# A fused attention and expert kernel: the two layers of each expert run back to back, and rows are loaded three experts ahead

## The chip, the cores and the metric

One core of a Trainium2 chip runs the whole program. The metric is the device time of one execution in microseconds (us), lower is better. TensorE is called PE in the profile (PEld is its weight load), VectorE DVE, ScalarE ACT, GpSimd POOL and SyncE SP.

## The reference

Three stages follow one another; the change touches the third.

```python
def _moe2_ref(x, w_skip, w_gate, w1, w2):      # x: 2304 tokens x 512, 8 experts, w1 512x1024, w2 1024x512
    do_compute = x @ w_skip > 0
    out = x.copy()
    xc = x[do_compute]
    logits = xc @ w_gate
    e_idx = np.argmax(logits, axis=1)
    probs = ...                                 # softmax of logits
    gate_w = probs[np.arange(len(xc)), e_idx]
    for e in range(E):
        mask = e_idx == e
        h = np.maximum(xc[mask] @ w1[e], 0.0)
        y[mask] = gate_w[mask, None] * (h @ w2[e])
    out[do_compute] = xc + y
    return out

def reference(**kwargs):
    attn_out = _attn_ref(...)                   # attention of 4 batches, 8 heads, local and strided masks
    x = _moe_ref(x=attn_out, w_in, w_out)       # x @ w_in, gelu-like gate, @ w_out
    return _moe2_ref(x=x, ...)
```

## The kernel before

The attention and the dense layer fill the first 585 us of the trace, with the routing of each group of tokens behind its dense layer. The routing scatters every token's row (512 numbers, its gate and its token number) by an indirect DMA of POOL into `xs_d` (L709), in a bin of 160 rows for its expert, and its number into a table (L710). The second stage, from about 585 us on, is the expert stage, and the change lies in it.

**One expert** e has five kinds of work. `load_x(e)` (L926) reads its 160 rows back from `xs_d`, as two halves of 80 rows, by two DMAs of SP (L929); each waits until the scatters have landed. `emit_X(e, cp)` (L933) transposes them on PE (L940), four transposes of 80 rows for each half `cp` of the columns, and DVE copies the result out to `xs[e]` (L944). `emit_L1(e, m)` (L946), for m of 0 to 7, multiplies with `w1` (L954) into a PSUM tile, and ACT takes the ReLU to `hT[e]` (L955). `emit_L2(e, c)` (L957), for c of 0 to 3, multiplies `hT[e]` with `w2` over its eight blocks (L963), and DVE copies the result to `yT[e]` (L966). `emit_Y(e)` (L968) transposes back on PE (L973), DVE multiplies by the gate and adds the row (L975), and POOL scatters the result rows to the output by an indirect DMA (L978). In the program's text each float32 product of L954 or L963 is one matmul; in the trace it is two, so that a layer of an expert is 32 products or 64 traced matmuls. Expert 0 has no `emit_X`: its rows are built on PE out of what is on the chip already (`xs0`).

**Weights.** A layer's weights are four loads of 512 KB on SP's queue (L202 for `w1`, L204 for `w2`). `wseq` (L183) is the order of the layers, and `wjobs` numbers the 64 loads by it, from 0 to 63; `wfill` (L208) issues them some layers ahead (`WD = 5`). Each goes into one of 33 buffers that the earlier stages use too. From load 14 on (`LG = 14`) a load is issued behind the first row loads (`issue_after`, L199).

**Order.** The lines emit the work in program order, and a scheduler then places instructions of each engine by its own estimate of times, so that the order on an engine can differ from the text. Before the change `wseq` is layer 1 of expert 0, layer 1 of expert 1, layer 2 of expert 0, layer 1 of expert 2, layer 2 of expert 1 and so on: layer 2 of an expert stands behind layer 1 of the next. The loop at L1005 walks through it; behind L1 piece 1 of expert e it emits `emit_Y(e - 2)` and `load_x(e + 2)`, and behind pieces 4 and 6 the two halves of `emit_X(e + 1)`. The rows of experts 1, 0, 2 and 3 are loaded ahead of the loop (L1000 to L1003).

Of the kernel before, what the change touches and what calls it, by code (L numbers as in the profile page):

```python
# [19 lines left out]
E, FF = 8, 1024  # L20
# [43 lines left out]
def attn_moe_moe_kernel(ctx: ExitStack, tc: tile.TileContext, q, k, v, w_in, w_out, w_skip, w_gate, w1, w2, out):  # L64
# [115 lines left out]
            wo[i] = w.rearrange("p (h n) -> p h n", h=2)  # L180


    wseq = [(0, 0)]  # L183
    for e_ in range(E):
        if e_ + 1 < E:
            wseq.append((e_ + 1, 0))
        wseq.append((e_, 1))
    wjobs = [(e_, l_, i_) for e_, l_ in wseq for i_ in range(4)]
    wx = {}
    nx = [0]  # L190
# [17 lines left out]
    def wfill(n):  # L208

        while nx[0] < min(n, len(wjobs)):  # L210
            wx_load()
# [3 lines left out]
    def after_scatters(ins, l_):  # L215

        for o_ in l_[SF - 1 :]:
            tc.add_manual_dep(
                ins, o_.ins.name, mybir.DependencyInfo(mybir.DependencyClass.Sync, mybir.DependencyReason.DATA), reason="every scatter has landed"
            )  # L220
# [701 lines left out]
    with ExitStack() as ph2:  # L922
# [3 lines left out]
        def load_x(e):  # L926
            for h in range(2):
                t = mp.tile([128, DM + 2], F32, tag="xr", bufs=8, name="xr")
                xl.append(nc.sync.dma_start(out=t[0:HC, :], in_=xs_d[e * CAP + h * HC : e * CAP + h * HC + HC]))  # L929
                after_scatters(xl[-1].ins, scat)  # L930
                xr[e, h] = t

        def emit_X(e, cp):  # L933

            if cp == 0:
                xs[e] = mp.tile([128, NC, CAP], F32, tag="xs", name="xs")
            tp = ps.tile([128, 2, CAP], F32, tag="t", bufs=2, name="tx")
            for c in range(2):
                for h in range(2):
                    nc.tensor.transpose(  # L940
                        out=tp[:, c, HC * h : HC * h + HC], in_=xr[e, h][0:HC, 128 * (2 * cp + c) : 128 * (2 * cp + c) + 128],
                        identity=ident[0:HC, 0:HC],
                    )
            nc.vector.tensor_copy(xs[e][:, 2 * cp : 2 * cp + 2, :], tp)  # L944

        def emit_L1(e, m):  # L946
            if m == 0:

                hT[e] = [half_tile(F32, "hT")[:, 0 : 4 * CAP].rearrange("p (k n) -> p k n", k=4) for _ in range(2)]
            tag = L1T0[m] if e == 0 else ("h", "sc", "h", "pv")[m % 4]  # L950
            p = ps.tile([128, CAP], F32, tag=tag, bufs=2 if tag == "h" else 1, name="h1")
            for c in range(NC):
                x = xs[e][:, c] if e else xs0[0][:, c]
                nc.tensor.matmul(out=p, lhsT=wx[e, 0, c][:, 128 * m : 128 * m + 128], rhs=x, start=(c == 0), stop=(c == NC - 1))  # L954
            nc.scalar.activation(out=hT[e][m // 4][:, m % 4, :], in_=p, func=AF.Relu)  # L955

        def emit_L2(e, c):  # L957
            if c == 0:
                yT[e] = mp.tile([128, NC, CAP], F32, tag="yT", name="yT")
            p = ps.tile([128, CAP], F32, tag=L2T[c] if e >= E - 2 else f"acc{c % 2}", bufs=2 if e >= E - 2 and L2T[c] == "h" else 1, name="h2")  # L960
            for k_ in range(NF):
                o = 512 * (k_ % 2) + 128 * c
                nc.tensor.matmul(  # L963
                    out=p, lhsT=wx[e, 1, k_ // 2][:, o : o + 128], rhs=hT[e][k_ // 4][:, k_ % 4], start=(k_ == 0), stop=(k_ == NF - 1)
                )
            nc.vector.tensor_copy(yT[e][:, c, :], p)  # L966

        def emit_Y(e):  # L968
            res = mp.tile([HC, 2, DM], F32, tag="res", bufs=2, name="res")
            for h in range(2):  # L970
                p = ps.tile([HC, DM], F32, tag="t", bufs=2, name="yp")
                for c in range(NC):
                    nc.tensor.transpose(out=p[:, 128 * c : 128 * c + 128], in_=yT[e][:, c, HC * h : HC * h + HC], identity=ident)  # L973
                xe = xr.pop((e, h))
                nc.vector.scalar_tensor_tensor(  # L975
                    out=res[:, h, :], in0=p, scalar=xe[0:HC, 512:513], in1=xe[0:HC, 0:DM], op0=ALU.mult, op1=ALU.add
                )
                ys.append(nc.gpsimd.indirect_dma_start(  # L978
                    out=out, out_offset=bass.IndirectOffsetOnAxis(ap=xe[0:HC, 513:514].bitcast(U32), axis=0), in_=res[:, h, :], in_offset=None,
                    bounds_check=NT - 1, oob_is_err=False,  # L980
                ))
                if len(ys) > 1:
                    tc.declare_no_dep(ys[-1].ins, ys[-2].ins, reason="rows of different tokens")

        seq = [(0, 0)]
        for e in range(E):
            if e + 1 < E:
                seq.append((e + 1, 0))
            seq.append((e, 1))

        pc = ps.tile([128, E], F32, tag="pv", name="pc")
        nc.tensor.matmul(out=pc, lhsT=ones, rhs=ohacc[:, 0:E], start=True, stop=True)
# [12 lines left out]
        for i, (e, layer) in enumerate(wseq):  # L1005
            n = NF if layer == 0 else NC
            for z in range(n):
                if z % (n // 4) == 0:
                    wfill(4 * (i + WD) + z * 4 // n + 1)
                if layer == 0:  # L1010
                    emit_L1(e, z)
                    if z == 1:
                        if e >= 2:
                            emit_Y(e - 2)
                        if 2 <= e < E - 2:
                            load_x(e + 2)
                    if z in (4, 6) and e + 1 < E:
                        emit_X(e + 1, z // 2 - 2)
                else:
                    emit_L2(e, z)  # L1020
                    if (e, z) == (E - 1, 0):
                        emit_Y(E - 2)
        emit_Y(E - 1)


# [88 lines left out]
```

## Time and profile before

| | us |
|---|---|
| median of 3 runs | 758.82 (757.9 to 760.88) |
| the profiled execution | 758.55 |
| its span in the trace | 756.8 |
| PE busy in the span | 715.0 (94%) |
| DVE, ACT, POOL busy | 352.9, 340.1, 164.2 |
| bytes moved by DMA | 84.44 MB |

The span is the profiled execution from its first to its last traced instruction; 1.75 us of the execution's own time lie around it. A matmul's end is modelled, and a matmul's entry reaches into the next, so the distance from one start to the next is what a matmul costs; some matmul records are missing from merged rows. The row of the clock is the granted share of TensorE's clock: 1.00 is 2.4 GHz, 0.50 is 1.2 GHz.

### The profile page before, as it was taken

The numbers are of one execution on the slowest core, as the hardware profiler recorded it, in microseconds if no ns is written. First come the engines' busy times: TensorE is split into PE (matmuls) and PEld (weight loads), VectorE is DVE, ScalarE is ACT, GpSimd is POOL, SyncE is SP. The second block draws the span as 40 slices with busy tenths as digits, with TensorE's granted clock in tenths as the row PEclk, the third lists the DMA queues.
The fourth block names the chain that finished last, engine by engine and source line by source line (L and its number), as shares of the span: only waits on it lengthen the run. The fifth ranks groups of instructions, "written<-read, shape, count | busy, mean of one in ns | idle before, by whom it ended". The sixth has DMA issues, their size and how long they took to land.

```text
span 756.8 us, 14113 instructions
## 1 busy us (share of the span) xinstructions
PE 715.0 (94%) x4945; PEld 630.5 (83%) x4945; DVE 352.9 (47%) x1450; ACT 340.1 (45%) x1098; POOL 164.2 (22%) x226
## 2 busy tenths in 40 slices
PE   5879989999999999999999999999999799999993
PEld 3558877888788888888888889989988699999993
DVE  3698986354655565366556443353453011121111
ACT  4886695663665665456665442332441111011100
POOL 5376774023031103003110302002021000000001
PEclk9968999999999999999999999999999899999998
DMA  8999921311220412211100000100792599961001
GB/s 194 340 336 289 273 53 25 84 34 45 68 52 20 108 35 34 74 33 45 50 17 1 17 30 16 57 1 16 223 161 68 180 398 397 358 231 36 16 14 33
DMA packets 99056, 84.44 MB, mean 112 GB/s; under 512 B 63508, under 2 KB 78036, under 8 KB 98976
## 3 DMA queue, kind: packets, MB, share of 16 engines
q1 hardware_dynamic: 95680, 78.39, 35.4%
q0 software_dynamic: 3296, 5.05, 2.1%
q8 instruction: 41, 0.67, 0.4%
q14 instruction: 39, 0.32, 0.2%
HBM read 71.00 MB, written 17.68 MB: 117 GB/s over the span
## 4 chain that ended last, share of the span: by engine, by line
PE 67%; issue 15%; DMA 8%; ACT 5%; DVE 2%; SPq 1%; POOL 0%; POOLq 0%; ACTq 0%; DVEq 0%
PE h L561 26%; PE acc L588 26%; DMA wx<-in_moe_w_dram 4%; PE sc L399 4%; PE pv L464 3%; PE tp L442 2%; DMA out_dram<-res,xr 2%; ACT pt L417 2%; ACT kb L337 1%; PE p L357 1%; PE tr L618 1%; DMA tab_d<-rows,ix 1%; PE lc L632 1%; PE p L361 1%; SPq L929 0%
## 5 line engine op out<-in xcount | busy, mean ns | idle before, releaser
L561 PE MATMUL h<-xT,wsp 128*128 128x256 f32 x1728 | 245.8, 287 | 2.5 <-POOL wsp L176 0.7
L561 PEld LDWEIGHTS h<-xT,wsp 128*128 128x128 f32 x1728 | 229.3, 191 | 18.3 <-issue 2.1
L588 PE MATMUL acc<-wsp,ghl 128*128 128x512 f32 x816 | 227.3, 404 | 1.0 <-ACT wsp L175 0.5
L588 PEld LDWEIGHTS acc<-wsp,ghl 128*128 128x128 f32 x816 | 141.3, 188 | 26.7 <-issue 2.0
L427 POOL TENSOR_TENSOR pt<-pt,st 96x256 f32<-96x256 f32 (+3 forms) x88 | 50.2, 589 | 241.0 <-DVE st L424 88.6
L565 DVE SCALAR_TENSOR_TENSOR g<-g,h 128x256 f32<-128x256 f32 x144 | 59.9, 418 | 89.9 <-ACT g L564 86.2
L564 ACT ACTIVATE g<-h 128x256 f32<-128x256 f32 x144 | 54.6, 382 | 96.0 <-PE h L561 88.6
L577 ACT ACTIVATE ghl<-g 128x256 fp32r<-128x256 f32 (+1 forms) x144 | 58.1, 405 | 63.2 <-DVE g L565 56.5
L954 PE MATMUL h<-xs,wx 128*128 128x160 f32 x512 | 77.5, 305 | 0.0
L417 ACT ACTIVATE pt<-pt,st 96x128 f32<-96x128 f32 (+3 forms) x176 | 67.3, 386 | 14.2 <-DVE st L409 13.9
L955 ACT ACTIVATE hT<-h 128x160 f32<-128x160 f32 x64 | 19.4, 303 | 120.7 <-PE h L954 115.1
L954 PEld LDWEIGHTS h<-xs,wx 128*128 128x128 f32 x512 | 72.8, 195 | 0.0
L963 PE MATMUL h<-hT,wx 128*128 128x160 f32 x512 | 72.4, 299 | 0.0
L578 DVE TENSOR_TENSOR ghl<-g,ghl 128x256 fp32r<-128x256 f32 (+1 forms) x128 | 53.2, 416 | 37.8 <-ACT ghl L577 29.4
L963 PEld LDWEIGHTS h<-hT,wx 128*128 128x128 f32 x512 | 70.3, 190 | 0.0
L399 PE MATMUL sc<-kb,qT 128*96 128x256 f32 (+3 forms) x220 | 45.4, 331 | 4.9 <-ACT kb L337 4.6
L709 POOL DMA_INDIRECT xs_d<-rows,ix x18 | 18.1, 1006 | 133.9 <-DVE ix L706 41.3
L176 POOL TENSOR_TENSOR wsp<-wcv,wsp 128x512 fp32r<-128x512 f32 x32 | 41.0, 1284 | 24.6 <-ACT wsp L175 24.0
L978 POOL DMA_INDIRECT out_dram<-res,xr x16 | 14.6, 914 | 145.5 <-DVE res L975 103.0
L966 DVE COPY yT<-h 128x160 f32<-128x160 f32 x32 | 10.4, 325 | 75.7 <-PE h L963 75.7
L337 ACT ACTIVATE kb<-p 64x64 fp32r<-64x64 f32 (+3 forms) x58 | 39.7, 684 | 10.7 <-DVE qT L340 3.8
L399 PEld LDWEIGHTS sc<-kb,qT 128*96 128x96 f32 (+2 forms) x220 | 32.1, 177 | 11.3 <-issue 4.5
(151 smaller groups left out, 762.0 us busy)
## 6 DMA issues: line engine op xcount, KB each, us to landing
wx<-in_moe_w_dram SPq DMA_DIRECT2D x64, 512.0 KB
wraw<-in_moe_w_in_dram SPq DMA_DIRECT2D x16, 512.0 KB
wraw<-in_moe_w_out_dram SPq DMA_DIRECT2D x16, 512.0 KB
raw<-in_q_dram SPq DMA_DIRECT2D x32, 128.0 KB
raw<-in_k_dram SPq DMA_DIRECT2D x32, 128.0 KB
out_dram<-rows SPq DMA_DIRECT2D x16, 256.0 KB
xs_d<-zinit SPq DMA_DIRECT2D x1, 2570.0 KB
xr<-xs_d SPq DMA_DIRECT2D x16, 160.6 KB
```

Of the source, the lines that this page charges most:

```text
L337: nc.scalar.activation(out=d[0], in_=ops[-1][0], func=AF.Copy)
L399: nc.tensor.matmul(out=sc[0:qn, j, :, 0:kn], lhsT=qt[a][:, q0 : q0 + qn], rhs=kt[c][:, :, k0 : k0 + kn], start=(n_ == 0), stop=(n_ == len( ...
L417: nc.scalar.activation(out=P[0:qn, j, h, 0:kn], in_=P[0:qn, j, h, 0:kn], func=AF.Exp, scale=-1.0, bias=st[0:qn, 0, i : i + 1], accum_out=s ...
L427: nc.gpsimd.tensor_tensor(out=P[0:qn, j, :, 0:kn], in0=P[0:qn, j, :, 0:kn], in1=st[0:qn, 1, 2 * j : 2 * j + 2, None].to_broadcast([qn, 2, ...
L561: nc.tensor.matmul(out=hp_, lhsT=wi[m][:, a, c, :], rhs=x[z], start=(n_ == 0), stop=(n_ == 3 * NC - 1))
L564: nc.scalar.activation(out=g, in_=hp_, func=AF.Tanh, scale=0.851)
L565: nc.vector.scalar_tensor_tensor(out=g, in0=g, scalar=1.0, in1=hp_, op0=ALU.add, op1=ALU.mult)
L577: nc.scalar.activation(out=t[:, 0], in_=g[:, a:z], func=AF.Copy)
L578: (nc.gpsimd if gi == 0 else nc.vector).tensor_tensor(out=t[:, 1], in0=g[:, a:z], in1=t[:, 0].bitcast(F32), op=ALU.subtract)
L588: nc.tensor.matmul(out=acc[gi, i], lhsT=ghl[i][:, a, :], rhs=wo[m][:, z, :], start=(m == 0 and n_ == 0), stop=(m == NM - 1 and n_ == 2),)
L954: nc.tensor.matmul(out=p, lhsT=wx[e, 0, c][:, 128 * m : 128 * m + 128], rhs=x, start=(c == 0), stop=(c == NC - 1))
L963: nc.tensor.matmul(out=p, lhsT=wx[e, 1, k_ // 2][:, o : o + 128], rhs=hT[e][k_ // 4][:, k_ % 4], start=(k_ == 0), stop=(k_ == NF - 1))
```

## The change

`wseq` becomes layer 1, layer 2 of expert 0, then both layers of expert 1, and so on; the weight loads are numbered by it. In the loop `emit_Y(e - 1)` comes behind piece 2 of layer 1 of e, and `load_x(e + 3)` behind that; the two halves of `emit_X(e + 1)` come behind pieces 1 and 2 of layer 2 of e (2 and 3 for expert 0). An unused list `seq` goes.

```diff
-    wseq = [(0, 0)]
-    for e_ in range(E):
-        if e_ + 1 < E:
-            wseq.append((e_ + 1, 0))
-        wseq.append((e_, 1))
+    wseq = [(e_, l_) for e_ in range(E) for l_ in range(2)]
...
                 if layer == 0:
                     emit_L1(e, z)
-                    if z == 1:
-                        if e >= 2:
-                            emit_Y(e - 2)
-                        if 2 <= e < E - 2:
-                            load_x(e + 2)
-                    if z in (4, 6) and e + 1 < E:
-                        emit_X(e + 1, z // 2 - 2)
+                    if z == 2 and e >= 1:
+                        emit_Y(e - 1)
+                        if e + 3 < E:
+                            load_x(e + 3)
                 else:
                     emit_L2(e, z)
-                    if (e, z) == (E - 1, 0):
-                        emit_Y(E - 2)
+                    z0 = 1 if e else 2
+                    if z0 <= z < z0 + 2 and e + 1 < E:
+                        emit_X(e + 1, z - z0)
         emit_Y(E - 1)
```

After the scheduler, the order on every engine is the same in both kernels up to the third product of expert 0's sixth group, apart from which weights the loads 4 to 13 fetch; on POOL it is the same to the end. In the rows below, `h_7327` and the like are PSUM tiles, `xs_7215` is expert 0's `xs0`, `xr` the loaded rows, `hT` the hidden layer, `x4` four products in a row.

PE, before, from the last products of expert 0's layer 1 that need no new rows to the first of layer 2:

```order
L954 MATMUL h_7321<-xs_7215,wx 128x160 x2
L954 MATMUL h_7334<-xs_7215,wx 128x160
L940 MATMUL tx<-ident,xr 128x80
L954 MATMUL h_7334<-xs_7215,wx 128x160
L940 MATMUL tx<-ident,xr 128x80 x3
L954 MATMUL h_7342<-xs_7215,wx 128x160 x4
L940 MATMUL tx<-ident,xr 128x80 x4
L954 MATMUL h_7354<-xs_7215,wx 128x160 x4
L963 MATMUL h_7446<-hT,wx 128x160
L963 MATMUL h_7434<-hT,wx 128x160
L954 MATMUL h_7364<-xs,wx 128x160 x2
```

Here the transposes of expert 1's rows (L940) stand inside the sixth group of expert 0's layer 1.

PE, after, at the same place:

```order
L950 MATMUL h_7327<-xs_7215,wx 128x160 x2
L959 MATMUL h_7362<-hT,wx 128x160
L950 MATMUL h_7335<-xs_7215,wx 128x160 x4
L959 MATMUL h_7362<-hT,wx 128x160 x2
L950 MATMUL h_7341<-xs_7215,wx 128x160 x4
L959 MATMUL h_7350<-hT,wx 128x160 x7
L959 MATMUL h_7362<-hT,wx 128x160 x4
L959 MATMUL h_7350<-hT,wx 128x160
L959 MATMUL h_7362<-hT,wx 128x160
L936 MATMUL tx<-ident,xr 128x80 x8
L959 MATMUL h_7374<-hT,wx 128x160 x8
L959 MATMUL h_7393<-hT,wx 128x160 x8
```

Now they stand behind all of that layer and half of layer 2, as one piece of eight.

SP, before, around the rows of expert 4 (a transfer waits for the semaphore that the transfer eight places ahead of it on the queue raises, `DMAHW0` to `DMAHW7` in turn):

```order
L204 DMA wx<-in_moe_w_dram 128x2x512 [waits DMAHW0_49,PE_49]
L202 DMA wx<-in_moe_w_dram 128x1024 [waits DMAHW1_49,PE_49]
L929 DMA xr<-xs_d 80x514 [waits DMAHW2_49,DMASW0_49,DVE_49]
L929 DMA xr<-xs_d 80x514 [waits DMAHW3_49,DMASW1_49,DVE_49]
L202 DMA wx<-in_moe_w_dram 128x1024 [waits DMAHW4_49,PE_49]
```

Here the rows follow 39 of the 50 weight loads that stand behind the first row loads.

SP, after, at the same place:

```order
L198 DMA wx<-in_moe_w_dram 128x1024 [waits DMAHW0_49,PE_49]
L925 DMA xr<-xs_d 80x514 [waits DMAHW1_49,DMASW0_49,DVE_49]
L925 DMA xr<-xs_d 80x514 [waits DMAHW2_49,DMASW1_49,DVE_49]
L200 DMA wx<-in_moe_w_dram 128x2x512 [waits DMAHW3_49,PE_49]
L200 DMA wx<-in_moe_w_dram 128x2x512 [waits DMAHW4_49,PE_49]
```

Now they follow 38 of them, the last of which is load 51.

PE, after, from the end of a middle expert's layer 1 to the transposes for the next expert (`h_7779` and `h_7791` are the first two pieces of layer 2):

```order
L950 MATMUL h_7764<-xs,wx 128x160 x4
L950 MATMUL h_7770<-xs,wx 128x160 x4
L959 MATMUL h_7779<-hT,wx 128x160 x6
L959 MATMUL h_7791<-hT,wx 128x160
L959 MATMUL h_7779<-hT,wx 128x160
L959 MATMUL h_7791<-hT,wx 128x160 x3
L959 MATMUL h_7779<-hT,wx 128x160
L959 MATMUL h_7791<-hT,wx 128x160 x4
L936 MATMUL tx<-ident,xr 128x80 x8
```

The scheduler has put seven and three products of other operands ahead of the two products that need the last two pieces of the hidden layer.

## Rows read from the trace of the kernel before

**Rows 1.** Windows of the span: PE busy, its clock, DMA share, GB/s

```profile
580.00:590.00 10.00, 9.44 (x72) 9.06 (x71) 3.71 (x32) 2.26 (x8) 1.94 (x2) 1.00 0.17 39
590.00:600.00 10.00, 4.35 (x26) 4.10 (x25) 0.49 (x1) 1.21 (x4) 0.00 (x0) 0.81 0.52 130
600.00:610.00 10.00, 10.00 (x70) 9.96 (x69) 0.98 (x2) 1.82 (x6) 0.00 (x0) 0.85 1.03 377
610.00:620.00 10.00, 10.00 (x77) 10.00 (x76) 1.14 (x3) 1.52 (x5) 0.00 (x0) 1.00 1.04 397
...
640.00:650.00 10.00, 10.00 (x77) 9.97 (x77) 1.73 (x3) 1.82 (x6) 1.82 (x2) 1.00 1.04 398
```

**Rows 2.** Timeline of PE: start, length, line, count, idle before and its releaser

```profile
585.69 6.41 PE L954 MATMUL h<-xs,wx 128*128 128x160 f32 x46
...
597.75 0.36 PE L940 MATMUL tx<-ident,xr 80*128 80x80 f32 x1 [5.65 <-DMA xr<-xs_d]
```

**Rows 3.** Windows of PE alone, one us each: busy, clock, DMA share, GB/s

```profile
595.00:596.00 1.00, 0.00 (x0) 1.00 0.89 294
596.00:597.00 1.00, 0.00 (x0) 0.56 0.96 208
...
601.00:602.00 1.00, 1.00 (x7) 0.50 0.96 348
602.00:603.00 1.00, 1.00 (x5) 0.53 0.98 383
603.00:604.00 1.00, 1.00 (x10) 1.00 1.05 401
```

**Rows 4.** Timeline of PE later in the stage, and the ReLU of a group

```profile
622.81 0.98 PE L954 MATMUL h<-xs,wx 128*128 128x160 f32 x6
...
623.83 0.30 ACT L955 ACTIVATE hT<-h 128x160 f32<-128x160 f32 x1 [5.08 <-PE h L954]
...
667.69 1.04 PE L973 MATMUL yp<-ident,yT 128*80 128x128 f32 x8
668.57 6.69 PE L954 MATMUL h<-xs,wx 128*128 128x160 f32 x48
675.09 0.43 PE L963 MATMUL h<-hT,wx 128*128 128x160 f32 x2
675.36 0.72 PE L940 MATMUL tx<-ident,xr 80*128 80x80 f32 x8
675.92 3.19 PE L963 MATMUL h<-hT,wx 128*128 128x160 f32 x22
...
743.78 1.04 PE L973 MATMUL yp<-ident,yT 128*80 128x128 f32 x8
```

**Rows 5.** Groups by line, whole span: count, busy, mean ns, idle before

```profile
L954 PE MATMUL h<-xs,wx 128*128 128x160 f32 x512 | 77.5, 305 | 0.0
L963 PE MATMUL h<-hT,wx 128*128 128x160 f32 x512 | 72.4, 299 | 0.0
...
L940 PE MATMUL tx<-ident,xr 80*128 80x80 f32 x56 | 6.9, 248 | 5.7 <-DMA xr<-xs_d 5.7
```

**Rows 6.** Timeline of SP: start of the first issue and time to the last

```profile
555.72 2.46 SPq L202 DMA_DIRECT2D wx<-in_moe_w_dram  x2
...
593.78 3.70 SPq L929 DMA_DIRECT2D xr<-xs_d  x8
597.52 0.90 SPq L202 DMA_DIRECT2D wx<-in_moe_w_dram  x2
...
606.82 4.43 SPq L204 DMA_DIRECT2D wx<-in_moe_w_dram  x4
...
617.36 4.42 SPq L204 DMA_DIRECT2D wx<-in_moe_w_dram  x4
...
627.92 4.46 SPq L204 DMA_DIRECT2D wx<-in_moe_w_dram  x4
...
639.17 4.43 SPq L204 DMA_DIRECT2D wx<-in_moe_w_dram  x4
644.86 0.34 SPq L202 DMA_DIRECT2D wx<-in_moe_w_dram  x1
645.80 1.61 SPq L929 DMA_DIRECT2D xr<-xs_d  x2
```

**Rows 7.** Timeline of POOL: the output scatters of expert 0 and the last

```profile
627.87 0.93 POOL L978 DMA_INDIRECT out_dram<-res,xr  x1 [40.09 <-DMA wx<-in_moe_w_dram]
...
746.99 0.91 POOL L978 DMA_INDIRECT out_dram<-res,xr  x1 [0.30 <-issue]
```

More of the change, by code (lines that the diff above doesn't have):

```diff
@@ L983, in emit_Y @@
                     tc.declare_no_dep(ys[-1].ins, ys[-2].ins, reason="rows of different tokens")
[L985 to L989, printed above, removed]
         pc = ps.tile([128, E], F32, tag="pv", name="pc")
```

## The prediction

> **What bounds the kernel now.** I read the windows of the expert stage first, then PE's timeline, then SP's. The windows [rows 1] show PE filled from 600 us on, with one hole: between 590 and 600 us it is busy 4.35 of 10 us. PE's timeline gives the hole its name [rows 2]: the products of expert 0 run dense from 585.69 to 592.1 us, then PE stands for 5.65 us until 597.75, and what releases it is the landing of expert 1's rows, for the transposes of L940 are next in its order. The groups by line show no other idle at the products or the transposes of rows [rows 5]. The hole costs more than its length. The granted clock falls to 0.50 (1.2 GHz) at about 596.4, 4.3 us after PE stopped, and comes back at about 602.9, 5.2 us after PE resumed [rows 3]. In those 5.2 us PE does 2.6 us of work. So the place is worth 5.65 + 2.6 = **8.25 us**.
>
> Beyond it the stage is PE's own work. Start to start, 48 products of L954 take from 668.57 to 675.09, 0.1358 us each; eight transposes back take 0.88 (667.69 to 668.57), eight of rows 0.56 (675.36 to 675.92) [rows 4]. So 1024 traced products, eight times 0.88, seven times 0.56 and the last drain of 0.16 (1.04 less 0.88) make 139.06 + 7.04 + 3.92 + 0.16 = 150.2 us. From 585.69 to the end of the last transposes (743.78 + 1.04 = 744.82) there are 159.1. The difference, 8.9, is the 8.25 and 0.65 of seams between groups, which I leave as they are.
>
> **Part 1: layer 2 of expert 0 moves ahead of everything that needs expert 1's rows.** The row loads themselves are not moved: SP issues them at 593.78, behind the last scatters, in both kernels. What moves is the need. After the change 64 products of layer 1 and 32 of layer 2 of expert 0 stand ahead of the first transpose: 585.69 + 96 x 0.1358 = 598.73 us. The rows were there at 597.75 at the latest, so the wait ends 1.0 us too early to be felt, and without the hole nothing lets the clock fall. Gain 8.25 us. The cover of this is expert 0's layer 2, and its weights must be there by 592 us. They are loads 4 to 7 now; the fourteenth load was issued by 558.2 [rows 6], 34 us earlier, and a load under full traffic takes 10.5 us (the issue at 617.36 waited for the one at 606.82, eight ahead of it). If they were not, the hole would be as before.
>
> **Part 2: layer 2 follows layer 1 of its own expert.** This adds a chain, PE, ReLU on ACT, PE, at eight boundaries. ACT starts 0.04 us after a group's end and takes 0.30 (622.81 + 0.98, then 623.83) [rows 4]. After a middle expert's last group eleven products, 22 traced matmuls, stand ahead of the one that reads the last piece: 22 x 0.1358 = 3.0 us of cover over some 0.4. I take nothing; without cover it would be 8 x 0.4 = 3 us. Behind the transposes of rows stand 32 matmuls, 4.3 us, ahead of the layer that reads them, so DVE's copies are covered too. What DVE, ACT and POOL execute is the same in number, and the end behind PE (the last scatter at 746.99 [rows 7]) is the same chain.
>
> **Part 3: rows three ahead.** The rows of expert 4 come by SP's queue behind load 51, and this is where the next wait stands. SP has at most eight transfers out. Loads 24 and 40 were issued at 606.82 and 627.92, a pace of 1.319 us a load; the next eight took 11.25 us instead of 10.55, and in them ran the output scatter of expert 0 (627.87), so a scatter costs the stream 0.70 [rows 6, 7]. After the change the scatters of experts 0 and 1 are done ahead of load 44's issue: 606.82 + 20 x 1.319 + 2 x 0.70 = 634.6. It lands 10.55 later, at 645.15, and lets the first half of the rows go. Seven loads are still out: 7 x 1.319 = 9.23, the scatter of expert 2 in that time 0.70, and 160.6 KB of rows against 512 KB in 1.319 us make 0.41. That is 655.5, and 655.9 for the second half. PE's need: an expert costs 8.69 + 0.88 + 8.69 + 0.56 = 18.82; expert 0 ends at 603.64; experts 1 and 2, layer 1 of expert 3 with its transposes (9.57) and half of its layer 2 (4.35) give 655.2. With 0.2 us from landing to release (SP went on at 597.52, PE at 597.75 [rows 2, 6]), PE waits about **0.9 us**, too short for the clock if 4.3 us were needed above. Before the change this place was not tight: transposes and rows were farther apart. The ends for this wait: rows that land as quickly as the first did, 3.7 us from issue (593.78 to 597.5), would be there at 650 and cost nothing; if each scatter held the stream 2 us instead of 0.7, it would be 4.8. I take the 0.9, since the stretch is the same saturated one (DMA share 1.04 at 640 to 650 us [rows 1]). Experts 5 to 7 are not tight: by the same count the rows of expert 5 land at about 669 and are needed at 675.
>
> The Trainium skill, DMA: Bandwidth & Descriptors, section "Queues, rings and completion order", speaks against the moved loads: what SP issues takes its place in the same rings, and each engine consumes a ring in order. By that rule the rows of expert 4 come behind the seven loads, as I have counted, and the sum is 751.2; if the rule did not hold here they would overtake, and the sum would be 750.3. No row of before decides it, since nobody waited for those rows there.
>
> **The sum.** The profiled execution took 758.55 us, 0.27 under the median of 758.82. 758.55 - 8.25 + 0.9 = 751.2; on the scale of the median, about **751.4 us**.
>
> **The rivals.**
> A, no new wait: the rows of expert 4 are in time, 758.55 - 8.25 = 750.3. For it: an idle queue landed rows in 3.7 us. Against: the saturated stream.
> B, the hole closes but the clock falls all the same, or a second pause near the start follows: only 5.65 is gained and 0.9 paid, 753.8. For it: the margin at expert 1's rows is 1.0 us only. Against: in the trace the clock fell only behind a pause of 4.3 us.
> C, the chain at the boundaries is not covered: the bunch of matmuls signals late, and each of eight costs 0.5: 751.2 + 4 = 755.2. Against: ACT followed its group by 0.04 us.
> D, slower: the rows of expert 4 come much later than counted, because weights and three scatters share the engines worse than in rows 6. A wait there of 5.65 us with a clock that falls again eats the whole 8.25; it decides from a landing at 660.9, 5 us later than my count. At 663 us the time is about 761 and, if expert 5 follows, 763.
> E, the change does not do what it says: the hole returns in front of layer 2 because its weights or the first rows are late, 758.5. Against: 34 us of lead, and the 1.0 us margin.
>
> **How the numbers follow.** Forecast 0.46, A 0.31, B 0.08, C 0.07, D 0.04, E 0.04. About 0.5% (3.8 us) is what a measurement of this kernel can tell from no change. The forecast, A, B and half of C are faster by more than that (below 755.0): 0.88. The other half of C and E lie within it: 0.08. D is slower: 0.04. For the range, the runs of before spread from 0.9 below to 2.1 above their median; from A less 1 to B plus 1 it is 749.2 to 754.8, and it leaves out C in part, D and E.
>
> **What would show it.** In the profile after: no idle between 585.7 and 598 us and a clock of 1.00 there and to 605; the transposes of expert 1 at about 598.7; the boundaries between layers without idle; one wait of PE on rows at about 655 us, of 0 to 2.5 us, and none at expert 5; the last PE instruction's end near 737.5 instead of 744.8. I am wrong if the clock drops between 596 and 603 without a pause, if PE waits for weights in layer 2 of expert 0, or if the wait at expert 4 is above 4 us.

## The result and the profile after

| us | before | after |
|---|---|---|
| median, runs of one session | 759.65 (757.9 to 761.4, 6 runs) | 753.6 (751.25 to 754.68, 6 runs) |
| ratio to before | 1 | 0.991 [0.9891, 0.9929] |
| the profiled execution | 758.55 | 751.34 |
| expert stage, first product to the end of the last transposes | 159.13 (585.69 to 744.82) | 152.23 (585.38 to 737.61) |
| stage less the 150.2 of work counted in the prediction | 8.9 | 2.0 |

The kernel became 0.9% faster: 751.34 in the profiled execution against 751.2 by the sum, 753.6 in the median against the forecast of 751.4, inside the range of 749.2 to 754.8. The stage gave all of it, 6.9 us between the two profiles.

The windows of 10 us of the kernel after, in the columns of [rows 1] (time, PE, PEld, DVE, ACT, POOL, clock, DMA share, GB/s):

```profile
590.00:600.00 10.00, 10.00 (x80) 10.00 (x79) 1.44 (x4) 1.82 (x6) 0.00 (x0) 1.00 0.54 139
600.00:610.00 10.00, 10.00 (x77) 9.98 (x77) 2.05 (x4) 1.33 (x5) 0.93 (x1) 1.00 1.03 388
650.00:660.00 10.00, 8.67 (x67) 8.31 (x66) 1.83 (x5) 0.38 (x2) 0.00 (x0) 1.00 1.05 333
```

The hole of [rows 1] is gone: PE is busy all of 590 to 600 us, where it had 4.35, and the clock stays at 1.00, where it had 0.81 and 0.85. A new and smaller hole stands at 650 to 660.

PE's timeline of the kernel after (start, length, line, operation, count, and in brackets the idle time before it and what released it), first where the old pause stood ([rows 2]), then around the rows of expert 4, then the end:

```profile
585.38 6.68 PE L950 MATMUL h<-xs,wx 128*128 128x160 f32 x48
...
594.89 3.69 PE L959 MATMUL h<-hT,wx 128*128 128x160 f32 x26
598.42 0.72 PE L936 MATMUL tx<-ident,xr 80*128 80x80 f32 x8
598.98 4.55 PE L959 MATMUL h<-hT,wx 128*128 128x160 f32 x32
...
650.66 4.51 PE L959 MATMUL h<-hT,wx 128*128 128x160 f32 x32
656.22 0.26 PE L936 MATMUL tx<-ident,xr 80*128 80x80 f32 x1 [1.06 <-DMA xr<-xs_d]
656.75 0.70 PE L936 MATMUL tx<-ident,xr 80*128 80x80 f32 x7 [0.27 <-DMA xr<-xs_d]
657.29 4.55 PE L959 MATMUL h<-hT,wx 128*128 128x160 f32 x32
...
675.60 0.72 PE L936 MATMUL tx<-ident,xr 80*128 80x80 f32 x8
...
736.57 1.04 PE L969 MATMUL yp<-ident,yT 128*80 128x128 f32 x8
```

The transposes of expert 1 start at 598.42 with no idle ahead of them. The prediction put them at 598.73, and the stage began 0.31 earlier than before: to the hundredth where it said. The one wait is at the rows of expert 4. Start to start the 32 products at 650.66 take 32 x 0.1358 = 4.35 us, so PE was free at 655.0; the next products start at 657.29, and the transposes themselves need 0.56: 2.29 - 0.56 = 1.73 us lost. The row at 675.60 is expert 5, without idle.

SP's timeline of the kernel after, which answers to [rows 6] (start of the first issue, time to the last):

```profile
593.40 3.59 SPq L925 DMA_DIRECT2D xr<-xs_d  x8
...
605.17 4.80 SPq L198 DMA_DIRECT2D wx<-in_moe_w_dram  x4
...
639.18 4.18 SPq L198 DMA_DIRECT2D wx<-in_moe_w_dram  x4
644.72 1.37 SPq L925 DMA_DIRECT2D xr<-xs_d  x2
647.12 4.62 SPq L200 DMA_DIRECT2D wx<-in_moe_w_dram  x4
```

The first half of expert 4's rows was issued at 644.72 (forecast: 645.15, less the 0.31) and let PE go at 656.22, 11.5 us later. In the kernel before, the rows issued from 593.78 on into an empty queue had let PE go at 597.75, 4.0 us later [rows 2, 6].

Windows of 5 us of the kernel after, PE alone (time, length, PE busy, clock, DMA share, GB/s), early in the stage and where the rows of expert 4 pass:

```profile
620.00:625.00 5.00, 5.00 (x39) 1.00 1.06 392
625.00:630.00 5.00, 5.00 (x40) 1.00 1.02 401
...
650.00:655.00 5.00, 5.00 (x39) 1.00 1.05 321
```

The DMA engines are as full at 650 to 655 as before (1.05), but they move 321 GB/s in place of some 400. Experiment e3 below shows that this dip goes with the rows.

The groups by line of the kernel after, which answer to [rows 5] (count, busy, mean ns, idle before, releaser):

```profile
L959 PE MATMUL h<-hT,wx 128*128 128x160 f32 x512 | 72.8, 300 | 0.0
L950 PE MATMUL h<-xs,wx 128*128 128x160 f32 x512 | 72.5, 299 | 0.0
...
L936 PE MATMUL tx<-ident,xr 80*128 80x80 f32 x56 | 5.4, 234 | 1.3 <-DMA xr<-xs_d 1.3
```

Layer 1's busy time fell from 77.5 to 72.5, since none of its products ran at half clock. Neither layer has idle time ahead of it: the eight new boundaries between layers cost PE nothing.

### The profile page after: what moved, and what is told of

It reads as the page before. It is cut to its first block, busy times and chain, and to the rows that moved or that the text cites. A ratio compares the mean times of both kernels' runs of the same rounds, so it can differ in the third digit from the quotient of the medians.

```text
span 749.6 us, 14124 instructions
## 1 busy us (share of the span) xinstructions
PE 712.9 (95%) x4945; PEld 628.3 (84%) x4945; DVE 352.1 (47%) x1450; ACT 340.3 (45%) x1098; POOL 164.6 (22%) x226
## 4 chain that ended last, share of the span: by engine, by line
PE 65%; issue 17%; DMA 8%; SPq 4%; ACT 3%; DVE 2%; POOL 0%; POOLq 0%; DVEq 0%; ACTq 0%
PE h L557 27%; PE acc L584 26%; PE pv L460 3%; PE sc L395 3%; DMA wraw<-in_moe_w_in_dram 2%; DMA out_dram<-res,xr 2%; PE tp L438 2%; DMA wx<-in_moe_w_dram 1%; PE tr L614 1%; SPq L158 1%; PE p L353 1%; DMA raw<-in_q_dram 1%; DMA tab_d<-rows,ix 1%; PE lc L628 1%; ACT pt L413 1%
## 5 line engine op out<-in xcount | busy, mean ns | idle before, releaser
L950 PE MATMUL h<-xs,wx 128*128 128x160 f32 x512 | 72.5, 299 | 0.0
L950 PEld LDWEIGHTS h<-xs,wx 128*128 128x128 f32 x512 | 70.3, 190 | 0.0
## 6 DMA issues: line engine op xcount, KB each, us to landing
xr<-xs_d SPq DMA_DIRECT2D x16, 160.6 KB
```

## The experiments

The theory at the outset: the time of the stage is the 150.2 of PE's work, plus each pause at rows that are late, plus a half clock behind a long pause; nothing else of the new order matters. The rival: part of the gain comes from elsewhere in the order of experts 1 to 7, or the pause is worth more or less than 8.25 with its clock. Ratios are against the same session's runs of before, whose median was 759.7 for e1 to e4 and 759.59 for e5 to e8; the stage is that of the profiled execution, from its first layer 1 product to the end of its last transposes. The waits are the idle times that the timeline shows; a wait can cost PE more than that (1.33 shown and 1.73 lost in the kernel after).

| kernel | median (range, runs) | ratio to before | stage | waits on rows | half clock |
|---|---|---|---|---|---|
| before | 759.65 (757.9 to 761.4, 6) | 1 | 159.13 | 5.65 at expert 1 | yes |
| after | 753.6 (751.25 to 754.68, 6) | 0.991 [0.9891, 0.9929] | 152.23 | 1.33 at expert 4 | no |
| e1 | 758.05 (756.53 to 760.97, 8) | 0.9973 [0.9947, 0.9999] | 158.96 | 4.67 at expert 4 | yes |
| e2 | 762.56 (758.67 to 766.65, 10) | 1.0034 [1.0011, 1.0056] | 162.22 | 2.12 at expert 1, 3.31 at expert 4 | at expert 4 |
| e3 | 750.84 (750.09 to 751.43, 4) | 0.9883 [0.9867, 0.99] | 150.49 | none | no |
| e4 | 758.34 (757.43 to 762.51, 10) | 0.9981 [0.9958, 1.0003] | 157.21 | 4.77 at expert 1 | yes |
| e5 | 751.07 (750.18 to 752.57, 4) | 0.9882 [0.9866, 0.9899] | 150.78 | none | no |
| e6 | 757.6 (756.73 to 758.35, 6) | 0.997 [0.9958, 0.9983] | 157.23 | 2.46 at expert 1 | no |
| e7 | 760.52 (758.68 to 762.14, 10) | 1.0013 [1.0002, 1.0024] | 159.42 | 5.38 at expert 1 | yes |
| e8 | 758.76 (757.9 to 759.99, 10) | 0.9989 [0.9979, 1.0] | 158.07 | 4.41 at expert 4 | yes |

**e1: the kernel before with only expert 0's part of the change.** Both layers of expert 0 come first, then the old order of layers, with the old two experts of lead.

```diff
-    wseq = [(0, 0)]
-    for e_ in range(E):
+    wseq = [(0, 0), (0, 1), (1, 0)]
+    for e_ in range(1, E):
...
-                    if z in (4, 6) and e + 1 < E:
+                    if z in (4, 6) and 1 <= e and e + 1 < E:
...
                     emit_L2(e, z)
+                    if e == 0 and z >= 2:
+                        emit_X(1, z - 2)
```

> The kernel before, with only expert 0's two layers put back to back (its layer 2 and the transposes of expert 1's rows behind it); experts 1 to 7 stay in the old order. My theory: the gain lies in this one place, so the pause at 592 us and the half clock behind it go (8.25 us). PE then comes to the rows of expert 4 at about 653.3 us; they stand behind load 52, one load more than in the changed kernel but with one scatter fewer ahead, and land at about 656.6, so there a wait of about 3.3 us is left: stage (first product to the end of the last transposes back) 153.8 us instead of 159.1, time about 753.2. Rival, the order of all experts and of all weight loads makes the gain: the stage stays above 156 us and the time above 756.

Measured: 758.05 with a stage of 158.96, almost nothing gained. PE's timeline of e1 has no wait at expert 1 (its transposes at 599.98), but this at expert 4; the last row is a window of PE alone (length, busy, clock, DMA share, GB/s):

```profile
659.30 0.33 PE L940 MATMUL tx<-ident,xr 80*128 80x80 f32 x2 [4.39 <-DMA xr<-xs_d]
659.90 1.06 PE L940 MATMUL tx<-ident,xr 80*128 80x80 f32 x6 [0.28 <-DMA xr<-xs_d]
```

```profile
660.00:665.00 5.00, 5.00 (x22) 0.50 1.03 392
```

The expectation (a stage of 153.8, time 753.2) failed. By its numbers the run reads as the rival that the order of all experts makes the gain; e5 below, which gains all of it with the old order, rules that out. The kernel before shows what happened instead. In its own PE timeline the transposes of expert 4 run without idle, well after the rows came:

```profile
661.62 0.30 PE L940 MATMUL tx<-ident,xr 80*128 80x80 f32 x2
662.07 0.58 PE L940 MATMUL tx<-ident,xr 80*128 80x80 f32 x6
```

The rows issued at 645.80 [rows 6] would be there by about 657.3, if they took the 11.5 of the kernel after. The pause at expert 1 had hidden that. Once PE does not stand there, in e1 it wants the rows at 654.9, they come at 659.3, PE stands 4.39 us and the clock falls again: the old loss at another place. The expectation had counted a wait of 3.3 us there and no fall of the clock. This is what rival D describes, in a kernel that has only half of the change.

**e2: the kernel before with the pause filled.** 14 unused products (28 traced, 28 x 0.1358 = 3.8 us) ahead of expert 1's transposes, to ask what a short pause without a fall of the clock costs.

```diff
+            if (e, cp) == (1, 0):
+                for d_ in range(FILL):
+                    nc.tensor.matmul(out=tp[:, 0, :], lhsT=wx[0, 0, d_ % 4][:, 0:128], rhs=xs0[0][:, d_ % 4], start=(d_ == 0), stop=(d_ == FILL - 1))
```

> The kernel before, with 14 products of 128 by 160 that nobody reads (28 traced matmuls, 3.8 us) put on PE ahead of the transposes of expert 1's rows. They do no useful work and fill a part of the pause only; some 2.2 us of it are left. My theory, that the half clock behind the pause costs 2.6 us by itself and comes from the length of the pause: the clock reads 1.00 from 585 to 605 us, the 2.6 us come back though PE does more work, and a wait at the rows of expert 4 of about 1 us stands against it: time about 756.9, stage 157.5. Rival, the clock falls near there whatever PE does, or its fall costs nothing: stage 159 or more, time 758.5 to 759.5.

Measured: 762.56, 0.3% slower than before, where 756.9 was expected. PE's timeline of e2, and windows as above:

```profile
597.30 0.47 PE L944 MATMUL tx<-ident,xr 80*128 80x80 f32 x4 [2.12 <-DMA xr<-xs_d]
...
658.59 0.33 PE L944 MATMUL tx<-ident,xr 80*128 80x80 f32 x2 [3.08 <-DMA xr<-xs_d]
```

```profile
600.00:605.00 5.00, 5.00 (x41) 1.00 0.96 334
...
660.00:665.00 5.00, 5.00 (x26) 0.66 1.06 264
```

At expert 1 it went as written: 2.12 us left of the pause, no fall. But the rows of expert 4 are late again, 3.08 us, with a fall of the clock. The run tells nothing of the price of the first place by itself; e6 repeats it without the second wait.

**e3: the kernel after, with expert 4's rows ahead of the bulk.** Weight loads from number 30 on are held behind these rows' issue.

```diff
             if len(xl) == 8 and nx[0] >= LG:
                 st.enter_context(tc.issue_after(xl[1].ins))
+            elif len(xl) == 10:
+                st.enter_context(tc.issue_after(xl[9].ins))
```

> The changed kernel, with weight loads from 30 on held behind the row loads of expert 4, which so stand behind load 29 on SP's queue instead of load 51. My theory, that PE's wait at 655 us is the place of these rows in the queue: no wait of PE on rows at any expert, the stage is 150.5 us instead of 152.2, the time about 749.7 where the changed kernel's profile has 751.3. Rival, the wait comes from something else at that place (PSUM tiles, DVE's copies) or moves to the weights that are held back: stage 152 or more, time 751.3 or more.

Measured: 750.84, the stage 150.49. The stage is as expected; the time is 1.1 above the expected 749.7, as the stage of the profiled execution began at 586.32, 0.94 later than in the kernel after. SP's and PE's timelines of e3, and windows of PE alone:

```profile
616.34 1.32 SPq L927 DMA_DIRECT2D xr<-xs_d  x2
```

```profile
655.94 0.72 PE L938 MATMUL tx<-ident,xr 80*128 80x80 f32 x8
```

```profile
620.00:625.00 5.00, 5.00 (x39) 1.00 1.04 340
625.00:630.00 5.00, 5.00 (x40) 1.00 1.05 340
...
650.00:655.00 5.00, 5.00 (x39) 1.00 1.03 412
```

The rows are issued 28 us earlier and the transposes of expert 4 wait for nothing. The 152.23 - 150.49 = 1.74 us between the stages is the 1.73 lost at that place. The stage without a wait is within 0.3 of the 150.2 of work that the prediction counted from rows of before. With the rows the dip in GB/s has moved from 650 to 655 us to 620 to 630, at a full DMA share in both places: the rows take more of the engines' time for a byte than the weights do. This version is 1.2% faster than the kernel before; its median lies 2.8 us below that of the kernel after, which is from another session.

**e4: the kernel after, with the transposes of expert 1 back inside layer 1 of expert 0.**

```diff
                     emit_L1(e, z)
+                    if e == 0 and z in (4, 6):
+                        emit_X(1, z // 2 - 2)
...
-                    z0 = 1 if e else 2
-                    if z0 <= z < z0 + 2 and e + 1 < E:
+                    z0 = 1
+                    if e and z0 <= z < z0 + 2 and e + 1 < E:
```

> The changed kernel, with the transposes of expert 1's rows put back to where they stood before, inside expert 0's layer 1; all else as changed. My theory, that the place of these transposes carries the whole gain: the pause of 5.65 us at 592 and the half clock for some 5 us are back, PE comes to expert 4 some 8 us later and does not wait there, stage about 158.8, time about 758.2. Rival, a part of the gain comes from the order of the other experts: stage 153 to 156, time 752 to 755.5.

Measured: 758.34, the gain gone, the stage 157.21. PE's timeline of e4, and windows of PE alone of one us:

```profile
598.09 0.26 PE L936 MATMUL tx<-ident,xr 80*128 80x80 f32 x1 [4.77 <-DMA xr<-xs_d]
```

```profile
597.00:598.00 1.00, 0.00 (x0) 1.00 1.09 253
598.00:599.00 1.00, 0.91 (x5) 0.62 0.80 214
599.00:600.00 1.00, 1.00 (x6) 0.50 1.05 282
600.00:601.00 1.00, 1.00 (x5) 0.50 1.19 230
601.00:602.00 1.00, 1.00 (x9) 0.68 0.70 205
```

One placement brings back the pause and the half clock, with the rest of the change in place; and with PE late again there is no wait at expert 4. So without the new place of these eight transposes there is no gain; e1 shows that the place alone is not enough. The stage is 1.6 shorter than expected, as the pause was 0.9 us shorter than in [rows 2], and PE worked about 3.3 us at half clock instead of the 5.2 of [rows 3].

**e5: e1 with the rows from expert 4 on issued early.** The same kernel as e1, with one addition:

```diff
+            elif len(xl) > 8:
+                st.enter_context(tc.issue_after(xl[-1].ins))
```

> The kernel of e1 (only expert 0's layers back to back), with the weight loads held behind each expert's row loads from expert 4 on, so that these rows stand behind load 32 on SP's queue instead of load 52. My theory after e1: the gain of the first pause was there too, and was given back at the rows of expert 4 (a pause of 4.7 us and a half clock behind it). With the rows early both pauses are gone: stage 150.5 to 151 us, time about 750 to 751, clock 1.00 throughout. Rival, the old order of experts 1 to 7 has a cost of its own: stage above 153, time above 752.5.

Measured: 751.07, the stage 150.78. Windows of e5, in the columns of [rows 1]:

```profile
590.00:600.00 10.00, 10.00 (x76) 10.00 (x75) 0.00 (x0) 2.39 (x8) 0.22 (x1) 1.00 0.27 70
600.00:610.00 10.00, 10.00 (x79) 10.00 (x79) 2.09 (x6) 0.91 (x3) 0.00 (x0) 1.00 1.04 333
650.00:660.00 10.00, 10.00 (x77) 9.97 (x76) 2.05 (x4) 1.33 (x5) 0.91 (x1) 1.00 0.80 312
```

With the old order of experts 1 to 7 and the old lead of two experts it is as quick as e3. The title's two points, both layers of one expert in a row and rows three ahead, are thus not needed beyond expert 0; what counts here is that PE waits for no rows.

**e6: e2 with the same early rows.** The products of e2 and the addition of e5 together.

> The kernel of e2 (before, 14 unused products in the first pause, some 2.1 us of it left), with the rows from expert 4 on early as in e5. Now nothing else pauses, and the half clock is measured by itself: 150.5 of work, 3.8 of unused products and 2.1 of pause make a stage of 156.4 us against 159.1, time about 755.8: PE does 3.8 us more than before and ends 2.7 earlier. Rival, the half clock costs nothing or comes all the same: stage 159 or more, time 758.5 or more.

Measured: 757.6, the stage 157.23, where 755.8 and 156.4 were expected. PE's timeline and the windows of e6 in the columns of [rows 1]:

```profile
599.21 0.47 PE L946 MATMUL tx<-ident,xr 80*128 80x80 f32 x4 [2.46 <-DMA xr<-xs_d]
```

```profile
590.00:600.00 10.00, 7.54 (x58) 7.33 (x57) 0.28 (x1) 1.52 (x5) 0.00 (x0) 1.00 0.40 99
600.00:610.00 10.00, 10.00 (x80) 10.00 (x80) 1.68 (x4) 2.43 (x8) 0.00 (x0) 1.00 1.03 346
```

The clock stays at 1.00. 150.49 of work, 3.8 of unused products and 2.46 of waiting are 156.75, within 0.5 of the stage. PE does 3.8 us more than in e7 below, waits 2.92 less (5.38 less 2.46), and its stage is 2.19 shorter. So the half clock of e7 cost some 3.8 - 2.92 + 2.19 = 3.1 us: it has a price of its own, apart from the wait.

**e7: the kernel before with the early rows alone.** Only e5's addition.

> The kernel before, with nothing changed but the rows from expert 4 on early on SP's queue. My theory: nobody waited for them there, since PE was 8 us late from the first pause, so nothing is gained: stage 158.5 to 159.5 us, time about 758.5. Rival, the early rows help by themselves (the scheduler also moves their transposes ahead): time below 756.

Measured: 760.52, nothing gained. The stage of 159.42 is within the expected 158.5 to 159.5; the time is 2 us above the expected 758.5, as the stage of the profiled execution began at 587.62, 1.9 later than in the kernel before. PE's timeline of e7 and a window of PE alone:

```profile
599.41 0.37 PE L942 MATMUL tx<-ident,xr 80*128 80x80 f32 x1 [5.38 <-DMA xr<-xs_d]
```

```profile
600.00:605.00 5.00, 5.00 (x23) 0.50 1.02 291
```

So the early rows of e3 and e5 are worth something only where the pause at expert 1 is gone: 759.65 with neither, 760.52 with early rows alone, 758.05 with expert 0's part alone (e1), 751.07 with both (e5).

**e8: the kernel after, with two unused loads of 512 KB ahead of expert 4's rows**, a price test of rival D. The rows then also stand behind load 52 instead of 51, so that three transfers more are ahead of them.

```diff
+                        if e == 1:
+                            for j_ in range(NJ):
+                                jt = mp.tile([128, 1024], F32, tag="junk", bufs=NJ, name="junk")
+                                nc.sync.dma_start(out=jt, in_=w1[0, 128 * j_ : 128 * j_ + 128, :])
```

> The changed kernel, with two extra loads of 512 KB that nobody reads ahead of the rows of expert 4, and these rows behind load 52 instead of 51: three transfers more ahead of them, 3 x 1.32 = 4.0 us; PE's order is the same. My theory: PE's wait at expert 4 grows from 1.3 to about 5.3 us, the clock falls behind it as it did at 592 us in the kernel before and takes up to 2.6 us: stage 156 to 159 us, time 755.5 to 758.5. Rival, the rows do not wait for what is ahead of them on the queue: the wait stays under 2.5 us and the time under 753.5.

Measured: 758.76, the stage 158.07. SP's and PE's timelines of e8, and a window of PE alone:

```profile
649.17 1.67 SPq L926 DMA_DIRECT2D xr<-xs_d  x2
```

```profile
660.90 1.70 PE L937 MATMUL tx<-ident,xr 80*128 80x80 f32 x8 [4.41 <-DMA xr<-xs_d]
```

```profile
660.00:665.00 5.00, 3.97 (x18) 0.50 1.04 353
```

Three more transfers at 1.319 are 3.96 us by the count. The rows were issued 62.47 us behind the start of the stage (586.70) instead of 59.34, and PE's first wait at them is 4.41 - 1.06 = 3.35 us longer. The clock falls, and all but about 1 us of the gain is gone (the stage of before is 159.13): 758.76 is just above the expected 755.5 to 758.5. The rows let PE go 11.7 us after their issue, 11.5 in the kernel after. The Trainium skill, DMA: Bandwidth & Descriptors, section "Queues, rings and completion order", says that on each DMA engine the descriptors of a ring are consumed in order. The 11.5 and 11.7 us behind loads that are out, against 4.0 in an idle queue, agree with it.

**e9 to e11: three more profiles of the kernel after**, to ask why its runs spread over 3.4 us.

> The changed kernel once more, for a look at what parts its executions, which lie at 751.3 in two cases and at 753.4 to 754.7 in four, while the kernels without a wait at expert 4 (e3, e5) lie within 750.1 to 752.6. My theory: the wait at the rows of expert 4 is a little longer in the slower ones and the clock falls behind it, for up to 2.6 us. So a profile of 753 us or more shows a clock of 0.50 for some us behind 655, and one below 752 does not. Rival: the difference lies ahead of 585 us, then the stage is 152.2 us in both.

> As e9, a second look at the changed kernel: a profile of 753 us or more shows a fallen clock behind the wait at expert 4 and a stage above 154 us, one below 752 shows a clock of 1.00 there and a stage of about 152. Rival: the same stage in both.

> As e9, a third look at the changed kernel, with the same two readings: a time of 753 us or more with a fallen clock behind 655 us and a stage above 154 us, or a time below 752 without. Rival: the same stage in both.

Measured: 752.3, 753.48 and 754.46, with stages of 152.10, 154.23 and 152.53 that begin at 586.31, 585.46 and 588.08, and first waits of 0.91, 1.46 and 1.34 us at expert 4. All three are from one further session, in which a single run of the kernel before took 762.0. The expected sign, a fall of the clock in profiles of 753 us or more, came in e10 and failed in e11. In e10 the clock fell behind the wait; PE's timeline and windows of PE alone of e10:

```profile
656.70 0.26 PE L936 MATMUL tx<-ident,xr 80*128 80x80 f32 x1 [1.46 <-DMA xr<-xs_d]
```

```profile
658.00:659.00 1.00, 1.00 (x6) 0.51 1.05 389
659.00:660.00 1.00, 1.00 (x5) 0.50 1.05 397
660.00:661.00 1.00, 1.00 (x6) 0.50 1.09 363
661.00:662.00 1.00, 1.00 (x8) 0.79 1.01 256
```

Two sources of the spread, then. One is a fall of the clock behind the short wait in one profile of four: the stage of e10 is 154.23 - 152.23 = 2.0 us longer than in the kernel after, of which 0.3 is the longer wait (1.46 + 0.19 against 1.33) and 1.7 the clock. The other is a start of the stage that varies by 2.7 us, which lies ahead of the change. In e11, the slowest, only the second is there. Why the attention and the dense layer end at different times is not settled. The granted clock differs there too: it fell once more at about 190 to 193 us in nine of the thirteen profiles of this document, whose stages begin at 585.46 to 588.08, and not in before, after and e2, which begin at 585.25 to 585.69, nor in e5, which begins at 588.13.

## Why the prediction came out right

**What bounds the kernel: right.** The count of 150.2 us of work for the stage met 150.49 in e3 and 150.78 in e5, the two versions with no wait. The difference of 8.25 + 0.65 was therefore read rightly off the trace of before, and e4 puts most of it back by moving eight transposes. That the half clock is a term beside the pause is shown by e6 against e7.

**Part 1: right.** The pause and its half clock went; the transposes stand where 96 products put them. From 159.13 to 150.49 there are 8.64 us, against 8.25: the rest, 0.4, is less than the 0.65 that the prediction left as seams.

**Part 2: right.** No idle at any boundary between layers, so rival C's condition did not arise. e5, which has only one boundary of the new kind, gains nothing over e3 by lacking the rest.

**Part 3: the mechanism right, the size too small, and three readings wrong.** The wait at the rows of expert 4 came at the place and in the order forecast, and was the only one. Mis-sized was the term of 0.9: 1.73 us were lost. PE's need came when it was forecast (655.0 against 654.9). The rows took 11.5 us from their issue to the release of PE, where the sum counts 9.23 + 0.70 + 0.41 + 0.2 = 10.5. The term that the runs point to is the 0.41 for the rows themselves, which were priced at the pace of the weights. The prediction's own [rows 3] have 294 and 208 GB/s at 595 to 597 us, where rows pass, at DMA shares of 0.89 and 0.96, and at 650 to 655 the kernel after moved 321 GB/s instead of some 400: estimated from these, 5 x (1 - 321 / 400) = 1.0 us. It is not the scatter, for in e1 none was started in that time and the rows took 11.7. No run changes the size of the rows, so how much each term was off is not shown.

That the issue came at the forecast time (644.72 against 644.84 with the earlier start) was partly luck. Load 24 went out at 605.17, 1.3 us earlier than in the sum, and from there to the rows' issue the queue took 39.55 us instead of the 38.33 counted.

The 3.7 us of an idle queue, and the 0.2 from landing to release, rest on SP going on at 597.52. No run shows them as such: [rows 6] have SP issuing eight transfers for 3.70 us from 593.78, so SP went on at 597.52 because the issuing had ended, whether or not a landing had come. What the rows show is PE's release after 4.0 us.

Wrong was also "too short for the clock": in e10 the clock fell behind 1.46 us. The 4.3 us from [rows 3] was the delay at one place and no condition for a fall. Nor did the clock fall "only behind a pause of 4.3 us" in the trace of before, as the prediction has it against rival B. In the attention stage PE stood for 3.26 us until 44.25, and the granted clock was 0.82 in the mean of 40 to 45 us and 0.50 in that of 45 to 50: it fell at about 43.2, some 2.2 us after PE had stopped.

**The scale.** The sum said 751.2 for a profiled execution and 751.34 came. That is closer than the terms deserve: this execution is one of the two quickest of its six, its stage began 0.31 earlier, and 0.4 of seams that went too made up for half of the mis-sized wait. The median is 2.2 above the forecast of 751.4: 0.83 because the runs of before in the same session have a median of 759.65 and not 758.82, about 0.4 from the wait less the seams, and some 0.9 that is left. A fall of the clock as in e10 (1.7 us of clock where it comes) in part of the executions, or a later start of the stage, could make it; which of them did was not measured. The lower end of the range is 749.2, where A less 1 is 749.3; nothing hangs on it.

**The rivals.** A, no new wait, is what e3 is: 750.84, for a forecast of 750.3; the change as made is not it. B came true in part: in e10 the clock fell, but at expert 4 and not at expert 1. D's mechanism and price are shown by e8: a wait of 4.41 with a fall of the clock eats most of the gain. Its 4.41 is less than the 5.65 that the prediction asked for, and the stage is still 1.06 shorter than before's, as it should be by that price; but the time can hardly be told from that of before (0.9989 [0.9979, 1.0]), and the kernel after was three transfers away from it. D was given too little: nothing in the prediction measured how near that edge was, and e1, a smaller form of the same change, is at it. E did not happen.

## What to carry to other kernels

A pause that is removed early brings the engine to every later transfer sooner, so the loads behind it have to move too: here removing the pause alone (e1) gained 0.3% (ratio 0.9973 [0.9947, 0.9999]), with the next rows early 1.2%. A small load that PE will wait for belongs ahead of the bulk loads of its queue; behind seven of 512 KB it took 11.5 us, in an idle queue 4.0. Price a pause of TensorE together with the half clock that may follow it, and do not take one observed delay of the clock for a rule.

## What the runs showed of the hardware

In the expert stage the granted clock fell to 0.50 behind waits of 1.46 (e10), 3.08 (e2), 4.39 (e1), 4.41 (e8), 4.77 (e4), 5.38 (e7) and 5.65 us (before), and stayed at 1.00 behind 0.91 (e9), 1.06 (after), 1.34 (e11), 2.12 (e2, at expert 1) and 2.46 (e6). The length of a wait alone does not order them: 1.46 was followed by a fall and 2.46 was not. The attention stage says the same: at 190.4 us of e10 the clock fell to 0.50 where the longest waits of PE near it were 0.36 and 0.59 us, and in before, with waits of 0.36 and 0.58 at the same place, it stayed at 1.00. What else decides was not found out.

The fall came after PE had resumed in e10 (it resumed at 656.70, and the clock was 0.51 from 658 on) and in e2 (resumed at 658.59, the clock still 1.00 from 659 to 660), while in [rows 3] it came in the middle of the pause. It lasted from about 3 us (e10) to 7 us (e1), for a price of 1.5 to 3.5 us.

The first half of expert 4's rows (160.6 KB) took 11.3 to 12.1 us from issue to PE's release behind a full queue, in seven profiles (e9 11.3, after 11.5, e11 11.6, e1 11.7, e8 11.7, e10 12.0, e2 12.1), though by the prediction's count the loads, the scatter and the rows account for 10.5, and without the scatter for 9.8 (e1). While such rows pass, the DMA engines move less at the same share: 321 GB/s at 650 to 655 us of the kernel after, and 340 at 620 to 630 of e3, against some 400.
